# Storing the even and odd parts of a mixed batch apart, and letting the feed-forward's loads add them

## The chip, the cores and the metric

The kernel runs on one core of a Trainium2 chip. The core has five engines that run side by side, each through its own queue in order: PE (matrix products, with its weight loads shown as PEld), DVE (element-wise work and reductions), ACT (activations and copies), POOL (element-wise work, and the issue of transfers that add to their target), SP (the issue of plain transfers). Products land in PSUM, from which DVE and ACT read; everything else is computed in SBUF, and transfers move data between SBUF and the memory outside (DRAM). The metric is the device time of one execution in microseconds (us); lower is better.

## What is computed

The inputs are q, k and v of 8 batches, 8 heads, 576 tokens and 64 channels, and two weights of a feed-forward. Attention has two parts, whose sum is x (8 x 576 x 512): a pooled one over means of 4 tokens, whose result is repeated 4 times, and a local one in which a token sees its neighbours within 3 places. Then

```
X = np.fft.fft(x, axis=1)
X = np.fft.fft(X, axis=2)
mixed = np.real(X).astype(np.float32)
u = x + mixed
mu = np.mean(u, axis=-1, keepdims=True)
var = np.mean((u - mu) ** 2, axis=-1, keepdims=True)
un = (u - mu) / np.sqrt(var + 1e-06)
ch = np.maximum(un @ w_ch1, 0.0) @ w_ch2
return (u + ch).astype(np.float32)
```

The Fourier transforms over tokens and channels are the mixing. Its real part is, over the token index k, a part that is even about the middle and one that is odd: token k has even + odd, and the token mirrored about the middle has even - odd.

## The kernel before

**Two stages.** In the first, batch by batch, the kernel computes pooled attention (`Pooled`), local attention in 5 units a batch (`Unit`) and the mixing (`Mix`). In the second, the 8 x 576 = 4608 tokens are cut into 36 tiles of 128, 4 to a block, and each of 9 blocks goes through the feed-forward (`Block`): 16 slices f of the inner size, with a first product into `hps`, a ReLU split into two parts `hh` (ACT) and `hl` (DVE), and a second product into `acc`. All products are made with operands split into a high and a low part. The weights are decoded on the way, by ACT, POOL (lines 164 and 193) and DVE (lines 172 to 178), from the transfers `raw`.

**The mixing.** `Mix.mix(t, odd)` makes, for each of three slots t of token rows (128, 128 and 64 rows), the even part (odd = 0) and the odd part (odd = 1) in a PSUM bank each, with even and odd channels in separate halves. `even_out` (line 629) copies the even part to SBUF on ACT. `unfold` (line 636) then reads it and the odd part from PSUM on DVE, adds or subtracts, and writes o0 (first half of the tokens) or o1 (second half, mirrored), with the channels put back into order. `Mix.store` (lines 643 to 655) writes o0 and o1 to the DRAM tensor `um` of the batch, each in five transfers on SP: four strided ones (56 partitions by 3 or 2 slots, and the row at the edge of a slot) and the first four rows. Two other tensors of the same shape hold the rest of u: `ux` the local attention and `ud` the pooled one. The middle token, 288, is stored once, and the second half lies mirrored, in rows 289 to 575; the output is put back into order at the end.

**The loads of a block.** `Block.load(i, part)` fetches tile i: part 0 is a plain transfer of `um` on SP (line 727), parts 1 and 2 are transfers of `ux` and `ud` on POOL that add to the same SBUF tile `ut` (line 725). A tile that crosses the end of a batch is fetched in two transfers. Block n + 1 uses the buffers of block n - 1, so its loads wait until that block's result is stored (`out_dram<-ut`, line 810). Then come the statistics `st` (line 734), `rstd` (line 738, on POOL), the normalised tile `un` (line 745), PE's transposes `tpn` (line 753) and the split `unT` (lines 759 and 762).

**What sets the order.** Every step is entered in a list with a time (`at(t, ...)`), and the list is sorted; each engine's queue follows it. The times are in planned units, not microseconds: a batch has 20 of them. The tables `AT` give the offsets. For the loads of blocks 0 and 1 it is `AT["add"]`: part p of block 0 at 120 + 17.46 p (+ 4 a tile), of block 1 at its start + 2.29 + 3.72 p. The loads of blocks 2 to 8 stand at 6 + 0.5 i + 2.5 part after the start of the block that runs meanwhile, and the first tile's statistics at 12 (lines 894 to 899).

Of the kernel before, what the change touches and what calls it, by code (L numbers as in the profile page):

```python
# [8 lines left out]
F32 = mybir.dt.float32  # L9
# [40 lines left out]
    "first_norms": (1.77, 1.54, 6.94, 0.87),  # L50
    "second_norms": (0.62, 1.28, 3, 1.2),

    "add": (17.46, 2.29, 3.72),
}


# [1 line left out]

ROUND = 5
TILES = 4  # L60
WARM_UP = 40

TINY_HIGH = 1.125 * 2.0**-15
# [4 lines left out]
def kernel(  # L68
# [13 lines left out]
    nc = tc.nc  # L82
# [23 lines left out]
    dram = ctx.enter_context(tc.tile_pool(name="dram", bufs=1, space=DRAM))  # L106
    ud = [dram.tile([S + 1, DM], F32, name=f"ud{b}") for b in range(B)]
    ux, um = ([dram.tile([S + 1, DM], F32, name=f"{n}{b}") for b in range(B)] for n in ("ux", "um"))

    res = ctx.enter_context(tc.tile_pool(name="res", bufs=1))  # L110

# [402 lines left out]
    class Mix:  # L514
# [109 lines left out]
                        to, l, r, start=(bool(odd) and i == 0), stop=(i == 2), skip_group_check=True  # L624
                    )

        def even_out(self, t):
            even = self.even[t] = pf.tile([P, DM], F32, name="even", bufs=2)
            nc.scalar.copy(out=even[: slots[t][1]], in_=self.ps[t, 0])

        def unfold(self, t, minus):
            if t == 0:
                self.o[minus] = pf.tile([P, NSL, DM], F32, name=f"o{minus}", bufs=1)
            n = slots[t][1]
            even, ps = (x.rearrange("p (two n) -> p n two", two=2) for x in (self.even[t][:n], self.ps[t, 1]))
            nc.vector.tensor_tensor(  # L636
                out=self.o[minus][:n, t].rearrange("p (n two) -> p n two", two=2),
                in0=even,
                in1=ps,
                op=ALU.subtract if minus else ALU.add,  # L640
            )

        def store(self, to, xs):

            for o, r0, first in ((xs[0], 0, 0), (xs[1], HS, 1)):

                for n2 in range(2):
                    n, base = NSL - n2, r0 + n2 * STEP
                    for lo, hi in ((4, 60), (60, 61)):
                        dst = to[self.b][base + lo : base + hi, :]  # L650
                        dst = bass.AP(
                            tensor=dst.tensor, offset=dst.offset, ap=[dst.ap[0], [2 * STEP * DM, n], dst.ap[1]]
                        )
                        nc.sync.dma_start(out=dst, in_=o[n2 * W + lo : n2 * W + hi, :n, :])
                nc.sync.dma_start(out=to[self.b][r0 + first : r0 + 4, :], in_=o[first:4, 0, :])

        def plan(self):
# [28 lines left out]
            for i in range(NSL):  # L686
                u = t + first + step * 2 * i
                at(u, self.mix, i, 0)
                at(u + even, self.even_out, i)
                at(u + step, self.mix, i, 1)  # L690
                at(u + step + plus, self.unfold, i, 0)
                at(u + step + minus, self.unfold, i, 1)
            at(u + step + store, self.store, um, self.o)
            at(4 * (NPAIR * self.b + NPAIR - 1) + AT["local_steps"][-1] + AT["store_local"][0], self.store, ux, (xa, xb))

    NU = B * NPAIR
# [10 lines left out]
    class Block:  # L707
# [7 lines left out]
        def load(self, i, part):  # L715
# [3 lines left out]
            while g < e:  # L719
                b, k0 = g // S, g % S  # L720
                m = min(e - g, S - k0)
                r0 = P - (e - g)
                src = (um, ux, ud)[part][b][k0 : k0 + m, :]
                if part:
                    nc.gpsimd.dma_start(out=u[r0 : r0 + m], in_=src, accum_op=ALU.add)  # L725
                else:
# [150 lines left out]
    at(t_e, close_e)  # L877
    at(t_d, close_d)
    for i in range(TILES):
        for part in range(3):  # L880
            at(120 + AT["add"][0] * part + 4 * i, blocks[0].load, i, part)
            at(t_a + AT["add"][1] + 0.1 * i + AT["add"][2] * part, blocks[1].load, i, part)
        for x, t, (first, step, first_n, step_n) in (
# [7 lines left out]
    for n, f0, f1 in [(0, 0, ROUND), (1, 0, ROUND), (0, ROUND, NF)] + [(n, ROUND * (n == 1), NF) for n in range(1, NBLK)]:  # L891
        starts[n] = t
        t = blocks[n].plan(t, f0, f1)
        if f1 == NF and 0 < n < NBLK - 1:
            for i in range(TILES):
                for part in range(3):
                    at(starts[n] + 6 + 0.5 * i + 2.5 * part, blocks[n + 1].load, i, part)
                v = starts[n] + 12 + i * (t - starts[n] - 18) / TILES
                blocks[n + 1].prepare(i, v, v + 1)

# [156 lines left out]
```

## Time and profile before

| | |
|---|---|
| time of the runs, us | median 1201.57 (1199.37 to 1205.03, 3 runs) |
| the profiled execution, us | 1200.32, span 1198.5 |
| mean granted PE clock | 0.972 |
| first product of the feed-forward (`hps`), us | 376.69 |
| start of the last `hps` group, us | 1186.46 |
| moved by transfers | 130.40 MB, mean 109 GB/s |

The span begins with the first instruction. A row of the timeline gives start, duration, engine, line, operation, output <- inputs, shapes, the count of instructions merged into it, and in brackets the idle time of the engine ahead of it with what ended it. "SPq" is SP's queue, whose durations are those of issuing a transfer, not of the transfer. The page's chain of work that ended last has this list by line:

```profile
PE hps L782 32%; PE acc L802 11%; PE acc L800 11%; PE acc L801 11%; PE y L584 3%; DMA vsum<-in_vg_dram 2%; DVE w L535 1%; DVE o L636 1%; PE tpn L753 1%; DMA ux<-xa 1%; DVE xs L524 1%; PE av L462 1%; DVE sums L389 1%; DMA raw<-in_wq_dram 1%; PE sc L403 1%
```

Two thirds are products of the feed-forward; the rest is spread over many lines of the first stage.

### The profile page before, as it was taken

How to read it: one execution, taken by the hardware profiler on the slowest of the kernel's cores; microseconds unless marked ns; L12 is line 12 of the kernel's file. 1: busy time of each engine (PE TensorE's matmuls, PEld its weight loads, DVE VectorE, ACT ScalarE, POOL GpSimd, SP SyncE). 2: the span in 40 equal slices, each digit the busy share in tenths (PEclk: the TensorE clock that was granted, in tenths of full speed). 3: DMA queues.
4: the chain of work that ended last, by engine and by line, in shares of the span. 5: the costliest groups of instructions: out<-in, count | busy, mean ns of one | idle time of the engine just before them, and what ended most of it. 6: DMA issues, size and time to landing. Idle time of an engine off the chain costs nothing.

```text
span 1198.5 us, 20501 instructions
## 1 busy us (share of the span) xinstructions
PE 1128.4 (94%) x8224; PEld 949.5 (79%) x8224; DVE 590.6 (49%) x1234; ACT 363.7 (30%) x1054; POOL 307.7 (26%) x410
## 2 busy tenths in 40 slices
PE   4879988899976999999999999999999999999998
PEld 4768877888875788888888888888888888888887
DVE  3698999999878989632321321321321322222111
ACT  3556675667643444311111111111111111111010
POOL 2155436335547556320300200300200300200000
PEclk7889998999997999999999999999999999999999
DMA  8586777778868454160600600600600600600000
GB/s 270 176 249 200 223 227 232 196 226 277 204 159 200 103 161 125 60 141 1 141 1 1 141 1 1 141 1 1 141 1 1 141 1 1 141 1 1 36 1 36
DMA packets 61631, 130.40 MB, mean 109 GB/s; under 512 B 7560, under 2 KB 7688, under 8 KB 61280
## 3 DMA queue, kind: packets, MB, share of 16 engines
q1 hardware_dynamic: 48016, 99.30, 26.1%
q0 software_dynamic: 13520, 29.79, 14.3%
q8 instruction: 65, 1.06, 0.3%
q14 instruction: 30, 0.25, 0.1%
HBM read 90.13 MB, written 37.80 MB: 107 GB/s over the span
## 4 chain that ended last, share of the span: by engine, by line
PE 74%; DVE 11%; DMA 6%; issue 4%; POOL 2%; ACT 1%; SPq 1%; DVEq 0%; POOLq 0%; ACTq 0%
PE hps L782 32%; PE acc L802 11%; PE acc L800 11%; PE acc L801 11%; PE y L584 3%; DMA vsum<-in_vg_dram 2%; DVE w L535 1%; DVE o L636 1%; PE tpn L753 1%; DMA ux<-xa 1%; DVE xs L524 1%; PE av L462 1%; DVE sums L389 1%; DMA raw<-in_wq_dram 1%; PE sc L403 1%
## 5 line engine op out<-in xcount | busy, mean ns | idle before, releaser
L790 DVE SCALAR_TENSOR_TENSOR hl<-hps,hh 128x512 fp32r<-128x512 f32 x144 | 99.4, 691 | 463.0 <-ACT hh L786 463.0
L782 PE MATMUL hps<-unT,w1h 128*128 128x512 f32 x1152 | 311.6, 392 | 1.7 <-DVE unT L762 1.0
L782 PEld LDWEIGHTS hps<-unT,w1h 128*128 128x128 f32 x1152 | 215.1, 188 | 47.8 <-DVE unT L762 1.3
L786 ACT ACTIVATE hh<-hps 128x512 fp32r<-128x512 f32 x144 | 86.2, 598 | 543.4 <-PE hps L782 543.4
L800 PE MATMUL acc<-w2h,hh 128*128 128x512 f32 x576 | 226.4, 393 | 0.0
L802 PE MATMUL acc<-w2h,hl 128*128 128x512 f32 x576 | 225.1, 391 | 0.0
L801 PE MATMUL acc<-w2l,hh 128*128 128x512 f32 x576 | 225.0, 391 | 0.0
L782 PE MATMUL hps<-unT,w1l 128*128 128x512 f32 x576 | 155.2, 391 | 0.0
L782 PEld LDWEIGHTS hps<-unT,w1l 128*128 128x128 f32 x576 | 108.1, 188 | 23.8
L802 PEld LDWEIGHTS acc<-w2h,hl 128*128 128x128 f32 x576 | 108.2, 188 | 23.6
L800 PEld LDWEIGHTS acc<-w2h,hh 128*128 128x128 f32 x576 | 108.2, 188 | 22.8
L801 PEld LDWEIGHTS acc<-w2l,hh 128*128 128x128 f32 x576 | 108.2, 188 | 22.8
L738 POOL TENSOR_TENSOR rstd<-rstd,mhalf 128x1 f32<-128x1 f32 x36 | 20.4, 568 | 307.9 <-DVE rstd L737 306.9
L725 POOL DMA_DIRECT2D ut<-ux x40 | 35.7, 1106 | 205.7 <-DMA ut<-um 205.5
L421 ACT ACTIVATE sb<-sc,mx 128x64 f32<-128x64 f32 x320 | 70.0, 330 | 1.3
L403 PEld LDWEIGHTS sc<-qkT 64*64 64x64 f32 x1280 | 48.0, 146 | 3.8 <-issue 1.2
L462 PE MATMUL av<-vaug,pT 64*64 64x65 f32 x1280 | 46.7, 224 | 4.1 <-DMA vaug<-in_vw_dram 4.0
L762 DVE TENSOR_TENSOR unT<-tpn,unT 128x512 fp32r<-128x512 f32 x36 | 24.7, 687 | 51.3 <-ACT unT L759 51.3
L562 POOL TENSOR_TENSOR fl<-xeo,fh 128x512 fp32r<-128x512 f32 x32 | 44.8, 1401 | 13.7 <-ACT fh L559 13.7
L403 PE MATMUL sc<-qkT 64*64 64x64 f32 x1280 | 48.0, 230 | 0.0
L389 DVE TENSOR_REDUCE sums<-qkT 128x224 f32<-128x896 f32 (+4 forms) x48 | 43.2, 943 | 8.6 <-DMA qkT<-in_qk_dram 8.6
L462 PEld LDWEIGHTS av<-vaug,pT 64*64 64x64 f32 x1280 | 42.9, 140 | 5.4 <-DMA vaug<-in_vw_dram 4.5
(95 smaller groups left out, 1474.2 us busy)
## 6 DMA issues: line engine op xcount, KB each, us to landing
qkT<-in_qk_dram SPq DMA_DIRECT2D x40, 512.0 KB
raw<-in_wq_dram SPq DMA_DIRECT2D x64, 256.0 KB
vaug<-in_vw_dram SPq DMA_DIRECT2D x40, 260.0 KB
ud<-odt SPq DMA_DIRECT2D x16, 576.0 KB
out_dram<-ut SPq DMA_DIRECT2D x36, 256.0 KB
ut<-um SPq DMA_DIRECT2D x32, 256.0 KB
ut<-ux POOLq DMA_DIRECT2D x32, 256.0 KB, 5.7
ut<-ud POOLq DMA_DIRECT2D x32, 256.0 KB, 5.3
```

The costliest lines, as they stand in the source:

```text
L389: nc.vector.tensor_reduce(out=to, in_=x[:, :, a - g0 : e - g0], axis=AX.X, op=ALU.add)
L403: nc.tensor.matmul(sc[r, a * W : (a + 1) * W], self.qkT[r, 0, a // 2, o : o + W], self.qkT[r, 1, a // 2, o : o + W], start=False, stop=Tru ...
L421: nc.scalar.activation(out=self.sb[:, a], in_=self.sc[:, a * W : (a + 1) * W], func=AF.Exp, scale=0.125, bias=self.mx[:, a : a + 1],)
L462: nc.tensor.matmul(av[r, a, :], pT[r, 4 * hh + a], va[r, 4 * hh + a, :], start=True, stop=True)
L562: nc.gpsimd.tensor_sub(out=self.fl[:, t], in0=self.x[t], in1=self.fh[:, t].bitcast(F32))
L584: nc.tensor.matmul(y, l, r, start=(i == 0), stop=(i == len(mms) - 1))
L782: nc.tensor.matmul(hps, a[:, c, :], unT[:, x, c, :], start=(i == 0), stop=(i == len(mms) - 1))
L786: nc.scalar.activation(out=hh, in_=self.hps[f], func=AF.Relu)
L790: nc.vector.scalar_tensor_tensor(out=hl, in0=self.hps[f], scalar=0.0, in1=self.hh[f].bitcast(F32), op0=ALU.max, op1=ALU.subtract)
L800: nc.tensor.matmul(acc, hh, w2h, start=start, stop=False)
L801: nc.tensor.matmul(acc, hh, w2l, start=False, stop=False)
L802: nc.tensor.matmul(acc, hl, w2h, start=False, stop=stop)
```

## The change

The mixing no longer adds on DVE. `out(t, odd, minus)` copies the even part (o[0]), the odd part (o[1]) and the negated odd part (o[2]) out of PSUM on ACT, with the channels put into order on the way. The even part is stored to a new DRAM tensor `ue` of 289 rows, half a batch, and the odd parts to `um`, o[1] in the first half and o[2] in the second. A load of a block now has four parts: part 0 a plain transfer of `ue` on SP, parts 1 to 3 accumulating transfers of `um`, `ux` and `ud` on POOL. As the even part of a token in the second half is a row of the first half, a tile that crosses token 288 is fetched from `ue` in two transfers. The planned times of the parts stand closer: 9 in place of 17.46 for block 0, 2.5 in place of 3.72 for block 1, 1.5 in place of 2.5 for the others.

```
-    "add": (17.46, 2.29, 3.72),
+    "add": (9, 2.29, 2.5),
...
+PARTS = 4
...
+    ue = [dram.tile([S // 2 + 1, DM], F32, name=f"ue{b}") for b in range(B)]
...
-        def even_out(self, t):
-            even = self.even[t] = pf.tile([P, DM], F32, name="even", bufs=2)
-            nc.scalar.copy(out=even[: slots[t][1]], in_=self.ps[t, 0])
-
-        def unfold(self, t, minus):
+        def out(self, t, odd, minus):
+
+            i = 1 + minus if odd else 0
             if t == 0:
-                self.o[minus] = pf.tile([P, NSL, DM], F32, name=f"o{minus}", bufs=1)
+                self.o[i] = pf.tile([P, NSL, DM], F32, name=f"o{i}", bufs=1)
             n = slots[t][1]
-            even, ps = (x.rearrange("p (two n) -> p n two", two=2) for x in (self.even[t][:n], self.ps[t, 1]))
-            nc.vector.tensor_tensor(
-                out=self.o[minus][:n, t].rearrange("p (n two) -> p n two", two=2),
-                in0=even,
-                in1=ps,
-                op=ALU.subtract if minus else ALU.add,
+            nc.scalar.mul(
+                out=self.o[i][:n, t].rearrange("p (n two) -> p n two", two=2),
+                in_=self.ps[t, odd].rearrange("p (two n) -> p n two", two=2),
+                mul=-1.0 if minus else 1.0,
             )
 
         def store(self, to, xs):
 
-            for o, r0, first in ((xs[0], 0, 0), (xs[1], HS, 1)):
+            for o, r0, first in zip(xs, (0, HS), (0, 1)):
...
-                at(u + even, self.even_out, i)
+                at(u + even, self.out, i, 0, 0)
                 at(u + step, self.mix, i, 1)
-                at(u + step + plus, self.unfold, i, 0)
-                at(u + step + minus, self.unfold, i, 1)
-            at(u + step + store, self.store, um, self.o)
+                at(u + step + plus, self.out, i, 1, 0)
+                at(u + step + minus, self.out, i, 1, 1)
+            at(u + step + store, lambda: self.store(ue, [self.o[0]]))
+            at(u + step + store, lambda: self.store(um, [self.o[1], self.o[2]]))
...
-                src = (um, ux, ud)[part][b][k0 : k0 + m, :]
+                if part == 0:
+
+                    m = min(m, HS + 1 - k0) if k0 <= HS else m
+                    j = k0 if k0 <= HS else k0 - HS
+                    src = ue[b][j : j + m, :]
+                else:
+                    src = (um, ux, ud)[part - 1][b][k0 : k0 + m, :]
...
-        for part in range(3):
+        for part in range(PARTS):
...
-                for part in range(3):
-                    at(starts[n] + 6 + 0.5 * i + 2.5 * part, blocks[n + 1].load, i, part)
+                for part in range(PARTS):
+                    at(starts[n] + 6 + 0.5 * i + 1.5 * part, blocks[n + 1].load, i, part)
```

Three places show how the queues change. The first is ACT's queue at the mixing of one batch, first and second slot (`o_4460` is the even part, `o_4513` the odd one, `o_4515` the negated one; `sb` are the exponentials of local attention, `mxd` and `sd` belong to pooled attention). Before:

```order
L629 COPY even<-mix 128x512
L572 CAST z<-odt 128x2
L559 CAST fh<-xeo 128x512
L419 ACTIVATE mx<-mx 128x8
L421 ACTIVATE sb<-sc,mx 128x64 x8
L276 ACTIVATE mxd<-mxd 72x4
L281 ACTIVATE sd<-sp,mxd 72x144 x4
L629 COPY even<-mix 128x512
```

and now:

```order
L636 ACTIVATE o_4460<-mix 128x512
L575 CAST z<-odt 128x2
L562 CAST fh<-xeo 128x512
L422 ACTIVATE mx<-mx 128x8
L424 ACTIVATE sb<-sc,mx 128x64 x8
L636 ACTIVATE o_4513<-mix 128x512
L636 ACTIVATE o_4515<-mix 128x512
L279 ACTIVATE mxd<-mxd 72x4
L284 ACTIVATE sd<-sp,mxd 72x144 x4
L636 ACTIVATE o_4460<-mix 128x512
```

The two copies of the odd part stand behind the exponentials and ahead of pooled attention's; on DVE two additions at the same place go, and nothing else moves there.

The second is POOL's queue over the loads of one block, block 4, whose tiles are `ut_103` to `ut_106` before:

```order
L725 DMA ut_103<-ux_68 128x512
L725 DMA ut_104<-ux_68 128x512
L725 DMA ut_105<-ux_69 128x512
L725 DMA ut_106<-ux_69 128x512
L725 DMA ut_103<-ud_60 128x512
L725 DMA ut_104<-ud_60 128x512
L738 TENSOR_TENSOR rstd<-rstd,mhalf 128x1
L725 DMA ut_105<-ud_61 128x512
L725 DMA ut_106<-ud_61 128x512
```

and `ut_111` to `ut_114` now:

```order
L731 DMA ut_111<-um_76 128x512
L731 DMA ut_112<-um_76 128x512
L731 DMA ut_113<-um_77 128x512
L731 DMA ut_111<-ux_68 128x512
L731 DMA ut_114<-um_77 128x512
L731 DMA ut_112<-ux_68 128x512
L731 DMA ut_113<-ux_69 128x512
L731 DMA ut_111<-ud_60 128x512
L731 DMA ut_114<-ux_69 128x512
L731 DMA ut_112<-ud_60 128x512
L731 DMA ut_113<-ud_61 128x512
L744 TENSOR_TENSOR rstd<-rstd,mhalf 128x1
```

The first tile's `ud` stood behind four transfers and now stands behind seven, and tile 3's `um` has come between the first tile's `ux` and its `ud`.

The third is SP's queue at the fetch of block 6, ahead of which the old result is stored. Before:

```order
L810 DMA out_dram<-ut_106 128x512
L727 DMA ut_103<-um_78 128x512
L727 DMA ut_104<-um_78 128x512
L727 DMA ut_105<-um_78 128x512
L727 DMA ut_106<-um_79 128x512
```

and now:

```order
L816 DMA out_dram<-ut_114 128x512
L733 DMA ut_111<-ue_86 97x512
L733 DMA ut_111<-ue_86 31x512
L733 DMA ut_112<-ue_86 128x512
L733 DMA ut_113<-ue_86 128x512
L733 DMA ut_114<-ue_87 128x512
```

The first tile's 128 rows have become transfers of 97 and 31 rows.

## The prediction

> **What bounds the kernel now.** I read the page first (busy shares and slices), then the busy times per batch period, then the timeline of one block's loads.
>
> ```profile
> PE 1128.4 (94%) x8224; PEld 949.5 (79%) x8224; DVE 590.6 (49%) x1234; ACT 363.7 (30%) x1054; POOL 307.7 (26%) x410
> PE   4879988899976999999999999999999999999998
> DVE  3698999999878989632321321321321322222111
> DMA  8586777778868454160600600600600600600000
> ```
>
> There are two regimes. From the fourteenth slice on (13 x 30 = 390 us) PE is full and DVE mostly free: the feed-forward. Before that both are high. The next rows cut the front part at the `odt<-odt` transfer that ends each batch's pooled attention, so that a row is one batch period; after the length come busy times of PE, PEld, DVE, ACT and POOL, PE's granted clock, DMA share and GB/s.
>
> ```profile
> 94.80:136.20 41.40, 38.14 (x569) 33.89 (x569) 38.16 (x88) 27.59 (x98) 18.73 (x23) 0.96 0.80 230
> 136.20:180.25 44.05, 39.55 (x556) 35.02 (x556) 40.56 (x93) 29.12 (x102) 20.92 (x26) 0.96 0.76 220
> 267.10:305.60 38.50, 36.66 (x569) 33.06 (x564) 35.39 (x84) 25.92 (x92) 18.36 (x21) 1.00 0.86 256
> 305.60:344.60 39.00, 36.02 (x569) 32.75 (x565) 30.42 (x77) 26.16 (x94) 18.17 (x21) 1.00 0.72 176
> 344.60:376.70 32.10, 16.26 (x130) 14.26 (x124) 28.90 (x53) 9.40 (x22) 19.77 (x24) 0.73 0.67 190
> 368.52 1.08 PE L753 MATMUL tpn<-ident,un 128*128 128x128 f32 x4 [15.17 <-DVE un L745]
> ```
>
> DVE is busy 92% of the middle periods, PE 90 to 95% beside it, ACT 67%. In the last row PE waits 15.17 us for DVE: only there does DVE set the pace alone.
>
> The second bound is the load of a feed-forward block, one row per step, for block 4 (SP stores the old block and fetches `um`; POOL adds `ux`, then `ud`; DVE takes statistics and normalises; PE transposes).
>
> ```profile
> 660.92 2.13 SPq L810 DMA_DIRECT2D out_dram<-ut  x4
> 663.15 3.09 SPq L727 DMA_DIRECT2D ut<-um  x4
> 666.78 3.54 POOL L725 DMA_DIRECT2D ut<-ux  x4 [32.58 <-DMA ut<-um]
> 671.40 0.85 POOL L725 DMA_DIRECT2D ut<-ud  x1 [1.08 <-DMA ut<-ux]
> 677.97 0.69 DVE L734 BATCH_NORM_STATS2 st<-ut 128x6 f32<-128x512 f32 x1 [0.97 <-DMA ut<-ud]
> 679.80 0.55 DVE L745 TENSOR_SCALAR un<-ut,mv,rstd 128x512 f32<-128x512 f32 x1 [0.74 <-POOL rstd L738]
> 681.06 0.60 PE L753 MATMUL tpn<-ident,un 128*128 128x128 f32 x4
> ```
>
> Each step is released by the landing of the one before, from the moment the buffer is free (660.92): the event times 6 and 2.5 in the plan no longer decide. `un` ends at 680.35 and PE, which has not idled, reaches the transposes at 681.06: 0.7 us of slack in a chain of 20 us. So this load already stands at the edge of PE's path.
>
> **The change, part by part.** First, DVE loses the 48 additions, ACT gets 48 more copies.
>
> ```profile
> L636 DVE TENSOR_TENSOR o<-even,mix 128x512 f32<-128x512 f32 (+1 forms) x48 | 31.3, 688 | 0.8 <-PE mix L623 0.7
> L629 ACT COPY even<-mix 128x512 f32<-128x512 f32 (+1 forms) x24 | 14.1, 588 | 3.2 <-PE mix L623 3.1
> 273.29 1.30 DVE L636 TENSOR_TENSOR o<-even,mix 128x512 f32<-128x512 f32 x2
> 274.51 1.48 DVE L524 TENSOR_TENSOR xs<-xa,xb 128x512 f32<-128x512 f32 x1
> ```
>
> A pair takes 274.51 - 273.29 = 1.22 us of DVE's queue, three pairs 3.7 us a batch. ACT pays 6 x 0.588 = 3.5 us (the even copy stays one instruction; the pair-wise order of its reading is new for ACT, and I price it like the plain copy): ACT goes from 67% to about 77% and stays cover. Bounds of the gain: nothing, if PE's 90 to 95% is the real limit; 7 x 3.7 = 26 us if DVE alone is (batches 0 to 6; batch 7's mixing lies under the feed-forward). In the period from 94.80 PE leaves 3.3 us, from 267.10 only 1.8 us, and both queues are in order, so I take half, 2 us for each of batches 0 to 5, and the full 3.7 us for batch 6, whose additions lie in PE's 15 us gap: -16 us.
>
> Second, SP stores `ue` as well: five transfers more a batch, directly ahead of the two `um` stores, and behind them wait the loads of `vaug`.
>
> ```profile
> 290.45 2.32 SPq L654 DMA_DIRECT2D um<-o  x4
> 292.82 0.42 SPq L655 DMA_DIRECT2D um<-o  x1
> 295.16 4.12 SPq L654 DMA_DIRECT2D um<-o  x4
> 299.80 1.38 SPq L375 DMA_DIRECT2D vaug<-in_vw_dram  x2
> 305.59 1.10 PE L462 MATMUL av<-vaug,pT 64*64 64x65 f32 x32
> ```
>
> Five stores cost SP 2.7 to 4.6 us, so `vaug` is issued near 303.5 instead of 299.80, 2 us ahead of a product that needs it: a wait of up to 2.5 us a batch, part of it inside PE's idle time. With 0.6 MB more a batch on transfer engines at 0.72 to 0.86, I take +0.5 us for each of six batches: +3 us (bounds 0 and 15).
>
> Third, block 1's loads. POOL issues five more accumulating transfers ahead of the first of these rows; the last is SP's fetch for the same block.
>
> ```profile
> 374.95 4.42 POOL L725 DMA_DIRECT2D ut<-ux  x5
> 382.86 0.74 POOL L193 TENSOR_TENSOR w1l<-wt,w1h 128x256 fp32r<-128x256 f32 x1 [1.63 <-ACT w1h L189]
> 384.37 0.61 POOL L164 TENSOR_SCALAR wt<-wt 128x256 f32<-128x256 f32 x1 [0.78 <-ACT wt L159]
> 384.93 2.62 POOL L725 DMA_DIRECT2D ut<-ud  x3
> 359.06 2.74 SPq L727 DMA_DIRECT2D ut<-um  x5
> ```
>
> That is 4.4 us of POOL's queue, behind which stand the clamps and differences of the weight decoding that DVE and PE wait for; POOL idles 1.63 + 0.78 us in this stretch, and before block 1's first products DVE has one pair less to do (1.2 us). I take +3 us (0 to 5). Block 0's four extra loads are spread over 30 us of planned time in the front part: nothing, hidden beside DVE.
>
> Fourth, and largest, blocks 2 to 8: the chain of a load gets one more accumulation. The hop costs what an accumulation costs there.
>
> ```profile
> 666.80:671.40 4.60, 4.60 (x22) 3.69 (x21) 0.66 (x1) 0.60 (x1) 3.48 (x4) 1.00 0.89 191
> 671.40:678.00 6.60, 6.60 (x30) 5.35 (x29) 0.76 (x3) 0.60 (x1) 1.71 (x2) 1.00 1.05 177
> q0 software_dynamic: 13520, 29.79, 14.3%
> ```
>
> From issue to the release of the next step: 671.40 - 666.78 = 4.6 us, 677.97 - 671.40 = 6.6 us, and the transfer engines are full meanwhile (0.89, 1.05). By bytes, 14.3% of 1198.5 us for 29.79 MB is 5.75 us per MB, 6.0 us for a block's 1.05 MB. I take 4.8 us, near the first, since tile 0's `ux` is issued before tile 3's `um` and need not wait for the whole part. The closer planned spacing saves nothing, as landings decide. Against it stands PE's slack:
>
> ```profile
> 859.54 0.55 DVE L745 TENSOR_SCALAR un<-ut,mv,rstd 128x512 f32<-128x512 f32 x1 [0.74 <-POOL rstd L738]
> 860.29 0.60 PE L753 MATMUL tpn<-ident,un 128*128 128x128 f32 x4
> 1037.24 0.55 DVE L745 TENSOR_SCALAR un<-ut,mv,rstd 128x512 f32<-128x512 f32 x1 [0.74 <-POOL rstd L738]
> 1039.55 0.60 PE L753 MATMUL tpn<-ident,un 128*128 128x128 f32 x4
> ```
>
> 0.2 us in block 6, 1.8 us in block 8, about 1.0 on average. Behind PE's waiting transposes stand all its later products, which nothing else covers: 7 x (4.8 - 1.0) = +27 us (4.6 and 6.0 give 25 and 35).
>
> Fifth, `ue` holds half a batch, so a tile that crosses token 288 is fetched in two transfers: 97 and 31 rows in blocks 1, 3, 6 and 8, 33 and 95 in blocks 0, 2, 5 and 7. No load of that kind is in this trace. Bounds: nothing, if such rows spread over all engines like the 128 of other tiles; or, 97 and 31 being prime, no equal shares exist and one engine moves all rows in turn. This row is the DMA view between 574 and 592 us, while block 3 is loaded:
>
> ```profile
> q1 hardware_dynamic: 791, 1.39, 24.6%
> ```
>
> 0.246 x 18 us x 16 / 791 packets = 90 ns a packet, so 128 rows in turn take 11.5 us in place of 0.7. In block 6 this is tile 0: +10.8 us. In block 8 it is tile 1, whose `um` stands on POOL ahead of tile 0's `ux`: about +8. In block 3 it is tile 3, whose `um` stands ahead of tile 0's `ud`: about +6. In block 1 SP fetches at 359.06, and POOL adds from 374.95: 0. I take the upper end, +25 us, because every large transfer here has a row count with a large divisor (128, 72, 64, 56), and nothing shows unequal shares.
>
> The Trainium skill ("DMA: Bandwidth & Descriptors", section on why a DMA increments its semaphore by 16) speaks against the change here: the largest number up to 16 that divides the row count is the number of engines used, and 127 partitions get one. By that rule the sum keeps the 25 us; with rows spread freely it would lose them. No run so far shows it.
>
> **Sum**, on the profiled execution (1200.3 us, span 1198.5; the median of the runs is 1.3 higher): 1200.3 - 16 + 3 + 3 + 27 + 25 = 1242 us.
>
> **Rivals.** (a) The prime row counts cost nothing: 1242 - 25 = 1217. For it: the trace has no such load; against it: the equal shares above. (b) Faster: DVE was the only bound of the front part, the full 26 us are gained, and the extra accumulation hides, because the parts of four tiles overlap and only one 256 KB transfer (a quarter of 6.0, 1.5 us) lengthens tile 0's chain: 7 x 0.5 = 4, so 1200 - 26 + 4 = 1178. It decides once the hop falls under some 3 us. For it: DVE's 92%; against it: each step of block 4 is released by a landing, and the engines are full. (c) Even: DVE's full 26 us against 27 for the hops, the other parts nothing: 1201. (d) SP becomes the bound of the front part: the `vaug` wait at its full 2.5 us for six batches and no DVE gain but batch 6's: 1242 + 12 + 12 = 1266. For it: 15 transfers in a row on one queue; against it: SP then waits for the next batch's `odt` anyway. (e) The additions do not leave the path because ACT's copies come late and hold PSUM banks: the gain of 16 falls away, 1258; ACT's third of idle time speaks against it.
>
> **Chances.** Forecast 0.53, (a) 0.16, (b) 0.07, (c) 0.09, (d) 0.07, (e) 0.08. The forecast's own range is 1225 to 1256, from its bounds (hops 25 to 35, rows 22 to 27, front -26 to -8). The range given, 1207 to 1268, takes in (a), (d) and (e) and leaves out (b) and (c). 0.5% is 6 us, about what a measurement of this kernel can tell: faster by more 0.09 (b and a little of c), within it 0.08, slower 0.83.
>
> **What would show it.** This row is DVE's wait for the loads after 505 us (total, times, longest):
>
> ```profile
> DVE st L734 <- DMA ut<-ud: 4.7, 5, 1.5
> ```
>
> It should grow to over 30 us, and PE's transposes of blocks 2 to 8 wait for `un` at seven places, 3 to 5 us in most, over 8 in blocks 3, 6 and 8. If these three are like the rest, the fifth part is wrong. The batch periods should shrink by about 2 us with DVE near 85%; if they shrink by 3.7, PE was not the limit; if they do not, SP or ACT took the place, and `av` will wait for `vaug`. With no PE wait in the feed-forward the whole forecast is wrong, and the kernel is faster.

## The result and the profile after

| | before | after |
|---|---|---|
| median of the runs, us | 1201.44 (1199.37 to 1205.03) | 1315.64 (1312.52 to 1318.78) |
| ratio, 95% interval | 1 | 1.0962 [1.0937, 1.0986] |
| profiled execution, its span, us | 1200.3, 1198.5 | 1315.1, 1313.3 |

The change costs 114 us. The forecast was 1242 (range 1207 to 1268): the direction came as predicted, the size did not, by 73 us. The page of the changed kernel, against the rows that the prediction shows of before: busy shares, three engines' slices and PE's granted clock, the queue of the accumulating transfers, and the chain that ended last.

```profile
PE 1162.5 (89%) x8224; PEld 973.1 (74%) x8224; DVE 577.5 (44%) x1186; ACT 386.7 (29%) x1102; POOL 338.0 (26%) x450
PE   6898998796966999989599999899599899689998
DVE  3889788686784889422122222122121221122111
PEclk7899898897988899999799999899899999989999
q0 software_dynamic: 18768, 39.23, 17.5%
PE 60%; DMA 16%; DVE 9%; SPq 5%; issue 4%; POOL 3%; ACT 2%; POOLq 0%; DVEq 0%; ACTq 0%
```

PE's share fell from 94 to 89%, and the feed-forward, which was a row of nines, has notches of 5, 6 and 8, one a block. Beside the digits its clock row has notches too. 9.4 MB more are accumulated (29.79 before).

Four events cut both executions into stages: the transfer `odt<-odt` that ends the last batch's pooled attention, the first product `hps` of block 0, and the first store of block 0 (`out_dram<-ut`).

| stage, us | before | after | difference |
|---|---|---|---|
| front part, to the last `odt<-odt` | 344.6 | 368.0 | +23.5 |
| to the first `hps` | 32.1 | 26.7 | -5.4 |
| start of the feed-forward, to block 0's store | 132.8 | 153.3 | +20.5 |
| the rest, blocks 1 to 8 | 689.1 | 765.3 | +76.2 |

**The rest first.** The waits of DVE and PE after 549 us (total, times, longest), and then block 6's load: SP stores the old block and fetches `ue`, POOL adds `um` to it, PE reaches the transposes.

```profile
DVE st L740 <- DMA ut<-ud: 74.3, 7, 17.2
PE tpn L759 <- DVE un L751: 62.0, 7, 15.4
```

```profile
915.85 2.12 SPq L816 DMA_DIRECT2D out_dram<-ut  x4
918.06 6.28 SPq L733 DMA_DIRECT2D ut<-ue  x5
932.25 2.65 POOL L731 DMA_DIRECT2D ut<-um  x3 [43.12 <-DVE hl L796]
949.66 1.11 PE L759 MATMUL tpn<-ident,un 128*128 128x128 f32 x4 [13.52 <-DVE un L751]
```

PE, which never stopped in the feed-forward before, waits for `un` once in each of blocks 2 to 8, 62.0 us in all. The single waits are 4.3, 15.4, 3.3, 6.3, 13.5, 4.5 and 14.7 us: blocks 3, 6 and 8, those with the fetches of 97 and 31 rows, stand out. In block 6, 14.2 us pass from SP's first fetch to POOL's first addition. (The page puts this wait of POOL down to DVE, which had been done; the same wait in `e1` below is put down to the landing of `ue`.)

**The front part.** SP's queue at the end of batch 4's mixing (the fifth of eight groups of stores), and the product that needs what is loaded last there:

```profile
303.40 2.61 SPq L653 DMA_DIRECT2D ue<-o  x4
306.05 0.51 SPq L654 DMA_DIRECT2D ue<-o  x1
306.68 5.61 SPq L653 DMA_DIRECT2D um<-o  x4
312.33 2.50 SPq L654 DMA_DIRECT2D um<-o  x1
314.94 5.07 SPq L653 DMA_DIRECT2D um<-o  x4
320.05 1.40 SPq L654 DMA_DIRECT2D um<-o  x1
321.51 1.40 SPq L378 DMA_DIRECT2D vaug<-in_vw_dram  x2
326.38 0.92 PE L465 MATMUL av<-vaug,pT 64*64 64x65 f32 x12 [8.55 <-DMA vaug<-in_vw_dram]
```

The stores ahead of `vaug` take SP 18.1 us here (303.40 to 321.51) in place of 9.4 (290.45 to 299.80), and not only because there are 15 in place of 10: the `um` stores themselves took 2.3 and 4.1 us for four before and take 5.6 and 5.1 now. PE waits 8.55 us. This batch is the worst one. Over batches 0 to 5 the stores ahead of `vaug` take SP 13.3 us on average in place of 8.6, the `um` stores among them 7.7 in place of 6.5 (the eight large ones), and PE's waits for `vaug` behind them come to 11.5 us, 8.55 of them here; before there was none behind a store.

**The start of the feed-forward.** SP, ACT and PE while batch 6 is stored, block 1 is loaded and the weights are decoded:

```profile
381.50 0.83 SPq L152 DMA_DIRECT2D raw<-in_wq_dram  x2
382.38 7.04 SPq L733 DMA_DIRECT2D ut<-ue  x6
389.46 1.92 SPq L152 DMA_DIRECT2D raw<-in_wq_dram  x2
391.48 5.50 SPq L653 DMA_DIRECT2D ue<-o  x4
400.61 0.26 SPq L654 DMA_DIRECT2D ue<-o  x1
414.28 24.27 SPq L152 DMA_DIRECT2D raw<-in_wq_dram  x9
420.60 0.43 ACT L162 ACTIVATE wt<-raw 128x256 f32<-128x256 f32 x1 [14.11 <-DMA raw<-in_wq_dram]
425.79 0.80 PE L619 MATMUL mix<-signs,yz 128*128 128x512 f32 x1 [8.84 <-DVE hl L796]
```

Between two groups of raw weights SP spends 23 us (391.4 to 414.28) on batch 6's 15 stores (batch 7's follow at 459.64), ACT waits 14.11 us for the weights, and PE, whose queue is in order, stands 8.84 us: its next product waits for `hl`, which on DVE stands behind the decoding of these weights.

One trace a kernel carries these stages. `e1` and `e9` below are the same program up to block 1, and their front parts end at 375.5 and 370.5 us: a front part is read from one trace to some 5 us, no closer.

### The profile page after: what moved, and what is told of

Same layout as the page of the kernel before. It is cut to its first block, busy times and chain, and to the rows that moved or that the text cites. A ratio compares the mean times of both kernels' runs of the same rounds, so it can differ in the third digit from the quotient of the medians.

```text
span 1313.3 us, 20627 instructions
## 1 busy us (share of the span) xinstructions
PE 1162.5 (89%) x8224; PEld 973.1 (74%) x8224; DVE 577.5 (44%) x1186; ACT 386.7 (29%) x1102; POOL 338.0 (26%) x450
## 4 chain that ended last, share of the span: by engine, by line
PE 60%; DMA 16%; DVE 9%; SPq 5%; issue 4%; POOL 3%; ACT 2%; POOLq 0%; DVEq 0%; ACTq 0%
PE hps L788 23%; PE acc L806 8%; PE acc L807 8%; PE acc L808 8%; DMA ut<-ue 4%; SPq L653 3%; DMA ut<-ud 3%; DMA vsum<-in_vg_dram 2%; PE y L587 2%; DMA ut<-ux 2%; PE av L465 2%; PE sc L406 2%; POOL ut L731 2%; DMA vaug<-in_vw_dram 2%; PE tpn L759 1%
## 5 line engine op out<-in xcount | busy, mean ns | idle before, releaser
L806 PE MATMUL acc<-w2h,hh 128*128 128x512 f32 x576 | 232.9, 404 | 1.9 <-DVE ut L812 1.0
L808 PE MATMUL acc<-w2h,hl 128*128 128x512 f32 x576 | 230.6, 400 | 2.6 <-DVE hl L796 2.6
L807 PE MATMUL acc<-w2l,hh 128*128 128x512 f32 x576 | 230.9, 401 | 0.0
L806 PEld LDWEIGHTS acc<-w2h,hh 128*128 128x128 f32 x576 | 112.0, 194 | 26.8 <-ACT hh L792 1.8
L731 POOL DMA_DIRECT2D ut<-um x40 | 38.0, 1100 | 247.7 <-DMA ut<-ue 198.1
L759 PE MATMUL tpn<-ident,un 128*128 128x128 f32 x144 | 25.0, 304 | 72.0 <-DVE un L751 72.0
L759 PEld LDWEIGHTS tpn<-ident,un 128*128 128x128 f32 x144 | 19.3, 155 | 78.8 <-DVE un L751 65.0
L765 ACT CAST unT<-tpn 128x512 fp32r<-128x512 f32 x36 | 21.1, 587 | 141.1 <-PE tpn L759 141.0
L740 DVE BATCH_NORM_STATS2 st<-ut 128x6 f32<-128x512 f32 x36 | 24.7, 685 | 74.3 <-DMA ut<-ud 74.3
L406 PEld LDWEIGHTS sc<-qkT 64*64 64x64 f32 x1280 | 53.0, 159 | 4.4 <-issue 2.1
```

What stands on the lines that cost most here:

```text
L406: nc.tensor.matmul(sc[r, a * W : (a + 1) * W], self.qkT[r, 0, a // 2, o : o + W], self.qkT[r, 1, a // 2, o : o + W], start=False, stop=Tru ...
L759: nc.tensor.transpose(tp[:, c * P : (c + 1) * P], self.un[i][:, c * P : (c + 1) * P], ident)
L806: nc.tensor.matmul(acc, hh, w2h, start=start, stop=False)
L807: nc.tensor.matmul(acc, hh, w2l, start=False, stop=False)
L808: nc.tensor.matmul(acc, hl, w2h, start=False, stop=stop)
```

## The experiments

Fourteen kernels were run. All times are medians; the kernel before had medians of 1199.8 to 1202.0 beside them.

### What each part of the change costs: a ladder

`e3` keeps only the copies, `e2` adds the stores of `ue`, `e13` adds its loads in blocks 2 to 8, and the changed kernel adds those in blocks 0 and 1. The edits, in the order `e2`, `e3`, `e13`:

```diff
 # e2: no load of ue; um starts the load
-                    src = ue[b][j : j + m, :]
+                    return
-                if part:
+                if part > 1:
 # e3: as e2, and
-            at(u + step + store, lambda: self.store(ue, [self.o[0]]))
 # e13: the changed kernel, and
                     src = ue[b][j : j + m, :]
+                    if self.n in (0, 1):
+                        return
-                if part:
+                if part > (self.n in (0, 1)):
```

> The changed kernel without the loads of ue: the even part is stored but left out of the sum, the fetch of um starts a load and the accumulations of ux and ud follow, as in the kernel before. Hop theory (the loads of the blocks cost 76 us by the traces, the front part the rest): the transposes of blocks 2 to 8 wait 0 to 2 us each, and the time falls by 70 to 90 us to 1225 to 1245; the first product of block 0 stays near 394.8 us from the span's start (376.7 before), because the front part does not depend on these loads. Rival (the feed-forward is slower for another reason, the clock or the stores): above 1260.

> As the run without the loads of ue, and without its stores too: of the change only the copies by ACT in place of DVE's additions remain. SP theory (the five more stores a batch on SP's queue made the front part slower): the first product of block 0 comes at 360 to 372 us, earlier than the 376.7 of before, the batch periods are 2 us or more below those of before, and the time is 1180 to 1195. ACT theory (the copies come late on ACT's in-order queue and hold up its other work): the first product comes at 385 us or later and the time is 1210 or more.

> The changed kernel in which blocks 0 and 1 both leave out the even part. Block 1's load alone gave 13.8 us, block 0's alone nothing. If the two are independent: 1299 to 1305. If they stand in for one another (block 0's load is hidden only while block 1's holds the same queues), which would account for the 10 us of the 114 that the causes measured singly leave over: 1289 to 1297.

| kernel | median, us | ratio to before, 95% interval | step |
|---|---|---|---|
| before | 1200.75 | | |
| `e3`: copies by ACT, DVE without additions | 1204.97 | 1.0039 [1.0018, 1.0061] | +4.2 |
| `e2`: and the stores of `ue` | 1216.32 | 1.0120 [1.0075, 1.0164] | +11.4 |
| `e13`: and its loads in blocks 2 to 8 | 1294.90 | 1.0789 [1.0757, 1.0822] | +78.6 |
| the changed kernel: and its loads in blocks 0 and 1 | 1315.64 | 1.0962 [1.0937, 1.0986] | +20.7 |

The steps add up to the 114.9 us by construction. `e2` came out below its range: its first `hps` is at 388.4 us and not near 394.8, and the loads of blocks 0 and 1, which the expectation had put to nothing, go with it. `e3` lies outside both ranges: the additions are gone from DVE, and nothing is gained.

### Where DVE's relief went

The stretch from the first to the eighth `odt<-odt` in one row each (length; busy time of PE, PEld, DVE, ACT and POOL; granted clock, DMA share, GB/s), before and then `e3`:

```profile
54.88:344.58 289.70, 259.71 (x3907) 231.37 (x3906) 259.14 (x604) 188.29 (x666) 134.27 (x161) 0.96 0.77 219
```

```profile
52.18:350.62 298.44, 268.18 (x3907) 238.03 (x3906) 249.35 (x568) 204.59 (x702) 132.73 (x162) 0.93 0.75 214
```

DVE has 36 instructions and 9.8 us less, and the stretch is 8.7 us longer. PE does the same 3907 matmuls in 8.5 us more, at a granted clock of 0.93 in place of 0.96: that is the whole difference. What was won is PE's gap ahead of the first transposes, 10.0 us in place of 15.2.

DVE itself kept less than half of its relief: the 36 additions of this stretch took 23.5 us, and its busy time fell by 9.8. Its element-wise sums and differences (`xs`, `w` and `xeo`) became longer, from 66.1 us to 75.4 in `e3` and 76.8 in the changed kernel, for the same work. One of the rows, before and in the changed kernel (21 instructions; busy us, mean ns):

```profile
L535 DVE TENSOR_TENSOR w<-xm 128x255 f32<-128x255 f32 x21 | 11.8, 563 | 0.0
```

```profile
L538 DVE TENSOR_TENSOR w<-xm 128x255 f32<-128x255 f32 x21 | 17.1, 813 | 0.0
```

In the timelines such an instruction takes 0.41 to 0.42 us where no computing operation of POOL overlaps it, and 0.94 (before) and 1.31 us (`e3`) on average where one does; 6 of the 21 are overlapped before, 12 in `e3`. So part of what DVE gave up came back where its sums met POOL's work.

Two tests of why PE gained nothing. `e7` takes 24 of ACT's copies away again; `e10` puts products of the identity ahead of `yz`, where three of PE's waits had grown from 1.2 to 1.3 us before to 1.7 to 2.5 us in `e3`.

```diff
 # e7: e3, and
-                at(u + step + minus, self.out, i, 1, 1)
-            at(u + step + store, lambda: self.store(um, [self.o[1], self.o[2]]))
+            at(u + step + store, lambda: self.store(um, [self.o[1], self.o[1]]))
 # e10: e3, and
             y = self.yzp = bank("yz", 4)[:, :NK1]
+            for _ in range(8):
+                nc.tensor.matmul(y[:, :P], ident[:, :4], ident, start=True, stop=True)
```

> The run without the loads and stores of ue (1204.97 us), and in it the negated copy of the odd part is left out too (both um stores take o[1]): 24 copies of 0.6 us fewer on ACT, and still no additions on DVE. ACT theory (what DVE gave up came back as waits behind ACT's in-order copies): the batch periods shrink by 1 us or more and the time falls below 1197. Rival (neither DVE nor ACT sets the pace of the front part, PE and its chain of hand-overs do): 1201 to 1208.

> The run without the loads and stores of ue (1204.97 us), and in it 8 such products (1.2 us) ahead of each product yz, whose wait for DVE and POOL grew from 1.2 to 1.3 us (clock behind it 1.0) to some 2.5 us (clock 0.5 to 0.6) at several places. Clock theory for the front part (the relief of DVE comes back as lower granted clock of PE): the batch periods shrink by 1 us or more, 1192 to 1199. Rival (PE is simply full): the 8 times 1.2 us add, 1205 to 1214.

`e7`: 1201.02 us, 1.0004 [0.9981, 1.0028], 4 us below `e3`, where ACT's theory asked for 8 or more and shorter batch periods: its stretch of seven periods is 298.68 us, that of `e3` 298.44. So ACT's copies cost a few us at most, and not in the periods. (In `e7` the four rows of DVE's sums take 73.7 us, as long as in `e3`.) `e10`: 1204.57 us, 1.0031 [0.9997, 1.0064], the same as `e3`, and it settles nothing, since the work came behind the wait and not into it:

```profile
335.21 1.91 PE L602 MATMUL yz<-ident 128*4 128x128 f32 x16 [2.89 <-DVE xa L483]
```

The products write the very tile of PSUM whose release PE waits for here. That the lost time is PE's lower clock is shown; what lengthened the waits ahead of its slow stretches is open, and no run separates the longer sums of DVE from the other candidates.

### The stores on SP: their place or their bytes

`e4` puts one group of five stores into the kernel before; `e8` moves it behind the loads of `vaug` for batches 0 to 5; `e14` does the same with the stores of `ue` in the changed kernel. For batches 6 and 7, which have no such loads behind them, the stores stay ahead of the raw weights in both.

```diff
 # e4: before, and (store takes one or two sources)
+            at(u + step + store, lambda: self.store(ue, [self.o[0]]))
             at(u + step + store, self.store, um, self.o)
 # e8: e4, and
-            at(u + step + store, lambda: self.store(ue, [self.o[0]]))
+            at(pooled_end(self.b + 2) + 0.04 if self.b < B - 2 else u + step + store, lambda: self.store(ue, [self.o[0]]))
 # e14: the changed kernel, and
-            at(u + step + store, lambda: self.store(ue, [self.o[0]]))
             at(u + step + store, lambda: self.store(um, [self.o[1], self.o[2]]))
+            at(pooled_end(self.b + 2) + 0.04 if self.b < B - 2 else u + step + store + 0.05, lambda: self.store(ue, [self.o[0]]))
```

> The kernel before with one group of five stores more per batch on SP's queue, o[0]'s rows into a buffer that nobody reads, directly ahead of the um stores; copies, additions and loads as before. SP theory: the loads of vaug and raw behind the stores come late, the first product of block 0 moves from 376.7 to 390 us or later, and block 0's store by 25 us or more; the time is 1222 to 1245. ACT theory: SP's stores are hidden, at most 3 us: 1200 to 1205.

> The kernel before with the dummy stores of ue (1217.49 us), and these moved on SP's queue behind the two loads of vaug, directly ahead of the next odt transfer, where SP waits anyway; the same stores, the same bytes. Order theory (the stores cost because loads that PE needs stand behind them): 1200 to 1208. Rival, contention (the bytes cost, wherever they stand): 1213 to 1222.

> The changed kernel with the stores of ue moved on SP behind the loads of vaug, and nothing else. If these stores cost in the changed kernel what they cost without the loads of ue (11 us): 1302 to 1308. If the 10 us left over come from the stores of the last batches meeting the fetches of ue on SP: 1290 to 1299. If they come from neither: above 1310.

`e4` takes 1217.49 us, 1.0120 [1.0087, 1.0152]: 16.7 us for stores that nobody reads (a little under the range). `e8`, the same stores behind `vaug`, takes 1206.30, 1.0056 [1.0029, 1.0082]. PE's waits for `vaug` up to the first `hps` before, in `e4` and in `e8`:

```profile
PE av L462 <- DMA vaug<-in_vw_dram: 4.0, 2, 2.4
```

```profile
PE av L463 <- DMA vaug<-in_vw_dram: 12.7, 7, 6.0
```

```profile
PE av L463 <- DMA vaug<-in_vw_dram: 2.5, 2, 1.3
```

So two thirds of the cost (11 of 16.7 us) are what stands behind the stores on SP. The other 6 are not assigned: the two groups that stayed are in them, and so is whatever the bytes cost (in the profiled execution of `e8`, 3.6 us above that of before, the front part ends at 345.1 us against 344.6). In the changed kernel the same move gives less, 1308.86 us, 1.0911 [1.0873, 1.0948]: 6.8 us, between the ranges of two answers.

### The loads of blocks 0 and 1

```diff
 # e6: as e13, for block 1 alone: if self.n in (1,)
 # e12: as e13, for block 0 alone: if self.n in (0,)
```

> The changed kernel in which block 1 alone leaves out the even part: its load is one fetch of um and two accumulations as before, everything else is unchanged. Theory (block 1's loads cost at the transition, on SP ahead of the raw weights and on POOL ahead of the decoding's clamps): block 0's store moves from 548 to 525 to 535 us, and the time to 1292 to 1303. Rival (the transition is slow because of batch 7's five stores of ue on SP): 1310 to 1316.

> The changed kernel in which block 0 alone leaves out the even part: um is fetched by SP, ux and ud are added, as before. The causes measured so far (feed-forward 75, block 1's load 14, stores 11, copies 4 us) leave some 10 of 114 us. Theory (block 0's load, four fetches more on SP and five accumulations more on POOL within the last batches, costs them): 1302 to 1310, the first product of block 0 at 386 to 390 us. Rival (hidden, as the prediction had it): 1312 to 1319.

`e6` takes 1301.84 us, 1.0866 [1.0819, 1.0913]: the fourth part of block 1's load costs 13.8 us, and the stage from the first `hps` to block 0's store falls from 153.3 to 135.5 us (132.8 before). The batch whose stores stand in that stage is 6, not 7 as the expectation has it. `e12` takes 1315.56, 1.0932 [1.0889, 1.0976]: block 0's load alone costs nothing that can be told from the spread. Both together (`e13`) give 20.7, which is more than 13.8 + 0 and lies in the range for one standing in for the other. The traces do not bear that out: behind the front part `e6` and `e13` are alike (135.5 and 136.4 us to block 0's store, 769.8 and 765.9 from there), and the front part, in which they differ by 8.5 us, varies by 5 without any edit. So this stays open. `e6` takes the fetch off SP and the accumulation off POOL at once; how the 13.8 us split between the two queues was not measured, but for the rows below.

### Rows, hop and clock in blocks 2 to 8

`e1` cuts the fetches into pieces with large divisors, `e9` fills PE's wait in `e1` with work, and `e5` moves the wait's place.

```diff
 # e1: the changed kernel, and
                     m = min(m, HS + 1 - k0) if k0 <= HS else m
+                    m -= m % 16 if 16 < m < P else 0
 # e9: e1, and
             tp = self.tp[i] = bank("tpn")
+            for _ in range(24 if i == 0 and self.n > 1 else 0):
+                nc.tensor.matmul(tp[:, :P], ident, ident, start=True, stop=True)
 # e5: the changed kernel, and
-                v = starts[n] + 12 + i * (t - starts[n] - 18) / TILES
+                v = starts[n] + 22 + i * (t - starts[n] - 28) / TILES
```

> The changed kernel, with every fetch of ue of 97, 31, 33 or 95 rows cut into pieces of 96+1, 16+15, 32+1 and 80+15 rows; the same bytes, two transfers more per crossing tile. One-engine theory: 97 and 31 rows go through one transfer engine each; cut, the waits of PE's transposes for un in blocks 3, 6 and 8 (15.4, 13.5 and 14.7 us) fall to the 3 to 5 us of blocks 2, 4 and 7, a gain of some 30 us, and up to 10 more at the start of block 1, where SP's next stores stand behind such a fetch: 1275 to 1286 us. Rival, contention: these blocks are late because the transfer engines are full and the row count does not matter: within 5 us of 1315.6.

`e1` takes 1277.66 us, 1.0612 [1.0544, 1.0681]: 38 us less with two transfers more per crossing tile. PE's waits after 548 us, and block 6's fetch and first addition:

```profile
PE tpn L760 <- DVE un L752: 29.3, 7, 4.9
```

```profile
905.70 4.63 SPq L734 DMA_DIRECT2D ut<-ue  x7
911.26 2.65 POOL L732 DMA_DIRECT2D ut<-um  x3 [34.50 <-DMA ut<-ue]
```

From fetch to addition it is now 5.6 us in place of 14.2, and the seven waits are alike, 3.3 to 4.9 us. By the Trainium skill ("DMA: Bandwidth & Descriptors", the section on why a DMA increments its semaphore by 16) 97 and 31 rows go through one engine each and 96 and 16 through sixteen; the two traces agree with it by these times, and show no engine by itself. The stage from the first `hps` to block 0's store became 8.3 us shorter as well (145.0). The same stage takes 143.3 and 142.2 us in `e9` and `e11`, which have the cut rows too, and 150.1 to 153.3 in the four changed kernels with block 1's rows left whole (`e5`, `e12`, `e14` and the change itself). In `e1`'s own trace, the slowest of its four runs (1263 to 1282 us), the front part came out 7.5 us longer, so that block 0's store is at 547.3 against 548.0.

Waits of 29.3 us are left, but `e1` is 43.7 us behind before in blocks 1 to 8. In the windows behind two of its waits (3.4 us at 570, 4.9 at 639; the columns are those above) PE's clock, third number from the end, is low for some 4 to 6 us:

```profile
570.40:575.00 4.60, 4.60 (x16) 3.86 (x17) 2.56 (x6) 0.59 (x1) 0.74 (x2) 0.67 0.66 95
575.00:580.00 5.00, 5.00 (x24) 4.14 (x23) 0.85 (x2) 0.60 (x1) 0.00 (x0) 1.00 0.00 0
639.30:645.00 5.70, 5.66 (x16) 4.60 (x17) 1.28 (x2) 0.59 (x1) 0.23 (x1) 0.50 0.50 85
```

> The kernel with the cut fetches (1277.66 us), and in blocks 2 to 8 PE multiplies the identity by itself 24 times (0.15 us each, 3.6 us) directly ahead of the first transposes, where it waited 3.3 to 4.9 us for un; the results are overwritten. Clock theory (a wait of 3 us or more leaves PE at a granted clock near 0.5 for the next 5 us, some 2 us a block on top of the wait): the work fills the wait, the rest of the wait is 0 to 1.3 us, the clock behind it stays at 1.0, and the time falls by 10 to 14 us to 1263 to 1268. Rival (the 2 us a block are something else, and work that is put in only adds): 1276 to 1284.

`e9` takes 1268.43 us, 1.0553 [1.0526, 1.0580], 9.2 us less than `e1` with more for PE to do (just under the 10 to 14 expected). The 24 products (48 records) took 5.4 us, not 3.6: each covers the whole wait and about 1 us more. Behind them the clock stays at 1.00:

```profile
560.07 5.52 PE L760 MATMUL tpn<-ident 128*128 128x128 f32 x48
566.00:570.00 4.00, 4.00 (x20) 3.29 (x19) 2.17 (x5) 0.59 (x1) 0.56 (x1) 1.00 0.11 19
```

On average over the seven waits a block of `e9` takes 95.0 us, 89.6 as before plus 5.4; a block of `e1` 95.8, which is 89.6 plus a wait of 4.2 plus 2.1 more, the price of the slow clock. Over seven blocks that is the 43.7 us less the 29.3 of waits, some 14 us; in the changed kernel it is 76.2 less 62.0, 14 as well. (By the traces blocks 1 to 8 of `e9` are 6.1 us shorter than those of `e1`; the rest of the 9.2 lies in the stages ahead and in the spread of `e1`.)

> The changed kernel with one line of the plan moved: the statistics, normalisation and transposes of the next block are planned from 22 instead of 12 behind the start of the block before it, so PE reaches them some 20 us later. Place theory (the load chain of a block is longer by one accumulation and by the single-engine rows, and costs only because the transposes stand where the old chain ended; the products behind them could have gone ahead): PE's waits for un in blocks 2 to 8 vanish, each block takes 89.6 us as before, and the time falls by some 76 us, to 1235 to 1247. Rival (the chain of loads from block to block is itself the bound, so the transposes wait wherever they stand): the waits stay, 1290 to 1316.

`e5` takes 1240.71 us, 1.0342 [1.0307, 1.0378]: 75 us less by one line of the plan, with the prime row counts and the extra hop still in it. PE's whole wait for `un` after 550 us:

```profile
PE tpn L759 <- DVE un L751: 0.8, 1, 0.8
```

Each block takes 89.6 us again. The load chain was never a bound in itself; it was late for the place at which the transposes stood in PE's queue.

### The repairs together

`e11` is the changed kernel with the edits of `e1`, `e5` and `e14`.

> The changed kernel with three repairs together: fetches cut into pieces, transposes planned later, and the stores of ue moved on SP behind the loads of vaug. If the causes add (76 us of waits in the feed-forward, 11 us of stores, 8 us at the start of block 1): 1316 - 76 - 11 - 8 = 1221, so 1214 to 1228, still slower than before, because block 1's accumulations on POOL and the copies remain. If one cause had stood in for another: 1235 or more.

It takes 1221.70 us, 1.0162 [1.0124, 1.0200], within a us of the 1221 expected from the causes, and is still slower than before. The single repairs' gains do not add (38, 75 and 6.8 us would give 1196), because `e1` and `e5` both take away the waits of blocks 3, 6 and 8. That the sum fits so closely is in part luck: its 11 us for the stores were 6.8 in `e14`. By stages `e11`'s trace has before's 689.1 us in blocks 1 to 8; what is left are 19.0 us in the front part, less 5.4 in PE's gap, and 9.4 up to block 0's store. No version of this change that was run beats the kernel before.

## Why the prediction was wrong, step by step

The forecast failed at three terms that it put too low or the wrong way (DVE's gain, the stores, block 1's load) and at one that it did not have (PE's clock behind each wait); its two largest terms, the hop and the rows, were right in mechanism.

- **Bounds.** That the load of a block stands at the edge of PE's path held: everything put into it came out at the end, until `e5` took the transposes away from the edge. The prediction had the slack of the chain (0.7 us at one block) and did not ask what sets it; the place of the transposes in the plan did. "DVE is busy 92%" holds for three of the four periods shown; the last has 78% (30.42 of 39.00). The forecast's own range of 1225 to 1256 does not come out of the bounds beside it, which give 1227 to 1260 with the +3 and +3; the measured time is far outside either.
- **First, DVE's additions, -16: failed.** `e3` measured +4.2. The 3.7 us for batch 6 in PE's gap came (5.1). The 2 us for each of the other batches did not: "I take half" split the gain between two engines, where the lower bound, PE's 90 to 95%, was the answer. PE then even got slower, by its granted clock, and of DVE's 23.5 us 13.7 came back as longer work of its own, 9.3 of it in the sums that can meet POOL's. Why PE's waits grew is open. ACT stayed cover within the 4 us of `e7`.
- **Second, five more stores on SP, +3: right mechanism, wrong size.** 11.4 in the ladder, within the bounds of 0 and 15; 16.7 in `e4`, beyond them. The wait at `vaug` came, 8.55 us in one batch and not 2.5, where the eight large `um` stores behind the new ones took SP 10.7 us in place of 6.4, while the step priced the five new ones alone; in the other five batches it was 0 to 1.2 us. What slowed those stores is open.
- **Third, block 1's loads, +3: failed.** 13.8 by `e6`, 20.7 with block 0. The step counted POOL's issues and left SP out, and the fifth put the rows there at nothing: "In block 1 SP fetches at 359.06, and POOL adds from 374.95: 0". Behind these fetches on SP stand the stores of batch 6 and the raw weights, for which ACT, and PE after it, waited; and `e1` shows some 8 us of that to be the rows. Block 0's load on its own was hidden, as predicted.
- **Fourth, the hop, +27: the wait was right, its tail was missing.** The seven waits of `e1` are 4.2 us each, against 4.8 - 1.0 = 3.8; in `e2`, without the hop, PE waits for `un` in none of these blocks. Each wait leaves PE at a granted clock of 0.5 to 0.67 for some 5 us, 2.1 us a block, which the sum has nothing for: 43.7 in all.
- **Fifth, the prime rows, +25: right.** The three blocks were the late ones (in block 6, 8 and 3 the waits fell by 8.7, 10.6 and 10.5 us in `e1`, against 10.8, 8 and 6 in the sum), and cutting the rows gave 38 us by the medians, 32 of them in blocks 1 to 8 (the waits 62.0 to 29.3) and the rest, which the step put at 0, at the start of block 1. The upper bound was the right end.
- **Rivals.** (a) falls with `e1`, (b) and (c) with `e3`, which has no hop and gains nothing. (d) came in part, beside the forecast and not in its place: the `vaug` waits were 11.5 us, against 15 at (d)'s full price, and DVE's gain stayed at batch 6's. (e) does not hold as a cause of 16 us: 24 copies fewer on ACT gave 4 us and no shorter periods.
- **Signs.** DVE's wait for the loads (74.3 us) and PE's seven waits with three long ones came as described. DVE's share fell to 84% in `e3`, and the periods did not shrink; the prediction read that as SP or ACT taking the place, but `e3` has none of the new stores and `e7` half the new copies. It was PE, at a lower clock.

By size the shortfall of 73 us is: 20 from DVE's gain that did not come, 8 from the stores, 18 from the loads of blocks 0 and 1, 27 from blocks 2 to 8 (78.6 against 52: the clock 14, the rows 7, the rest in sizes).

## What to carry to other kernels

When a step is added to a load chain, look first at where its consumer stands in the in-order queue: here moving the transposes by one number undid 75 of 114 us, while making the chain itself shorter gave half as much. An engine relieved of work gives time only where it alone is waited for; at 92% beside a PE at 90 to 95% it gave none. And a transfer is priced with all that stands behind it on its queue, not by its own issue time.

## What the runs showed of the hardware

- **A short stop of PE cost about one and a half times itself here.** Waits of 3.3 to 4.9 us were followed by 4 to 6 us at a granted clock of 0.5 to 0.67 (4.2 us of wait, 2.1 more behind it), and shorter ones too: in the changed kernel the wait of 2.45 us at 297 is followed by 0.50, while before the wait at the same product was 1.29 us and the clock behind it 1.00 (windows of 4 us behind the wait, of after and of before):

```profile
297.05 1.23 PE L603 MATMUL yz<-seqm,z 128*4 128x320 f32 x4 [2.45 <-POOL z L576]
297.07:301.05 3.98, 3.98 (x26) 2.50 (x28) 3.78 (x7) 1.63 (x8) 2.85 (x3) 0.50 1.01 397
```

```profile
287.03 1.19 PE L600 MATMUL yz<-seqm,z 128*4 128x320 f32 x7 [1.29 <-POOL z L573]
287.05:291.03 3.98, 3.87 (x81) 3.15 (x81) 3.67 (x10) 2.75 (x12) 2.69 (x3) 1.00 0.91 314
```

  The Trainium skill ("TensorE: Matmul & The Clock Gate", HAM oscillation — how this bites in real kernels) asks for no idle gaps of PE beyond about 3.4 us. The direction agrees; here a gap of 2.45 us was enough. In the front parts of six traces (before, after, `e1`, `e3`, `e7`, `e8`), with the clock at 0.92 or more in the 4 us ahead of the wait, 39 of 40 waits of 2.0 to 2.9 us were followed by 4 us at 0.50 to 0.77, 8 of 12 waits of 1.4 to 1.9 us by a lower clock too, and 30 of 32 waits of 1.0 to 1.3 us by 1.00.
- **Work that computes nothing can pay.** 5.4 us of products into a tile that is overwritten made a block 0.8 us shorter than the wait of 4.2 us in their place.
- **A fetch of 97 and 31 rows held back its queue.** Block 1's fetches took SP 3.87 us for eight in `e1` and 7.04 for six with the 97 and 31 rows among them; block 6's 4.63 for seven and 6.28 for five. Block 2's, with 33 and 95 rows, took 2.80 for five.
- **Sums on DVE met POOL.** A sum of 128 x 255 (`w<-xm`) took 0.41 us with POOL still and 0.94 to 1.35 on average with one of POOL's operations beside it (before, after and `e3`).
